# Uniform 128-row value matmuls, paired small matmuls and a planned order per engine in a fused sliding-window attention and token mixer

## Chip, cores and metric

The kernel runs on one core of one Trainium2 chip. The metric is the device time of one execution in microseconds (us), lower is better. Most figures are the median of several executions. An execution is called slow here when it is over 1.5% longer than the fastest of the same kernel.

## The reference

For 8 batches and 8 heads, with 576 tokens and 64 numbers a head, attention looks back over 128 tokens and has a bias that falls with distance. Its output, heads side by side, is `x` (576 x 512 for each batch), which goes through a token mixer.

```python
scores = scale * np.matmul(q, k.transpose(0, 1, 3, 2))
mask = (rel >= 0) & (rel < window)                     # window = 128
scores = np.where(mask, scores + bias[None], -1e9)
attn = softmax(scores)                                 # over the last axis
x = np.matmul(attn, v)                                 # then heads side by side: (8, 576, 512)

wq = x @ w_q                                           # 576 x 64
wk = x @ w_k                                           # 576 x 64
W_tok = scale * np.einsum('bsd,btd->bst', wq, wk)
mixed = np.einsum('bst,btd->bsd', W_tok, x)            # = scale * wq (wk^T x)
out = np.maximum(mixed, 0.0) @ w_out
```

Both kernels use the form in the last comment: `G = wk^T x` (64 x 512) first, then `wq G`. So no 576 x 576 matrix is made in the mixer.

## The kernel before

The kernel is software-pipelined by hand. Each unit of work is put on a list with a time; the list is sorted and issued in that order, and each engine then works through its own part strictly in order. The units of one batch, with the names used below:

- `c.q`, `c.k`, `c.v`: GpSimd casts the loaded fp32 data to fp16. `T` and `eT`: TensorE transposes q and k, and an eviction copies them out of PSUM.
- `QK.u` (8 a batch), `exp.u` on ScalarE, `mul.u` on VectorE: scores, exponent, and an in-place multiply with a table of the bias and mask.
- `PV.t` and `nrm.t` (5 a batch): values times weights for a tile of 128 queries, and the division on VectorE. The fifth tile has 64 tokens.
- `xT`, `wq`, `wk`, `G`, `mx`, `out`: the mixer, with evictions `exT`, `ewq`, `ewk`, `eG`, `emx`, `eo`. `st`: stores.

PSUM is used as four buffers of two banks each, shared by all these units.

```python
PERIOD = 16.0
...
    def pv_unit(b, qt, t):
        ...
            for h in range(H):
                o = 512 * (h // 4) + 65 * (h % 4)
                kts = ([qt - 1] if qt else []) + [qt]
                for i, kt in enumerate(kts):
                    g, c = P_AT[kt, qt]
                    kn = QT_N[kt]                       # 128, or 64 for the last tile of keys
                    nc.tensor.matmul(px[:n, o : o + 65], st["p", h, g][:kn, c : c + n],
                                     vb[:kn, kt, h, :],
                                     start=(i == 0), stop=(i == len(kts) - 1))
...
    def wk_unit(b, t):      # wk by tokens: transposes of the projection's eviction
        ...
                nc.tensor.transpose(pk[:n, 64 * i : 64 * i + 64],
                                    st["wqkT"][64:128, 128 * i : 128 * i + n],
                                    identh[64:128, 64:128])
...
    def g_unit(b, t):       # wk^T x, one matmul of 512 columns for each tile of tokens
        ...
                nc.tensor.matmul(pg[0:64, 0:512], st["wkn"][:n, 64 * i : 64 * i + 64],
                                 st["x", i][:n, :], start=(i == 0), stop=(i == NQT - 1))
...
    def mixed_unit(b, db, t, eng):   # four tiles, one after the other
        ...
            for lo, hi in ((0, 512), (512, S)):
                nc.tensor.matmul(pm[:, lo:hi], st["g"][:, 128 * db : 128 * db + 128],
                                 st["wqkT"][0:64, lo:hi], start=True, stop=True)
...
        for u in range(8):
            qk_unit(b, u, t0 + 2.0 * u)
        for qt, t in enumerate((10.4, 12.4, 18.4, 20.4, 22.4)):
            pv_unit(b, qt, t0 + t)
        ...                                             # times written by hand
```

The softmax here doesn't subtract the row's maximum and nothing guards it: scores larger than these inputs give would overflow.

## Time and profile before

| | before |
|---|---|
| median of 3 executions | 206.88 us (205.60 to 207.73) |
| span of the profiled execution | 209.2 us |
| TensorE busy | 170.2 us, 81% |
| VectorE busy | 145.4 us |
| ScalarE busy | 113.9 us |
| GpSimd busy | 86.5 us |

These lines are from the page of the kernel before: busy time by engine (PE is TensorE, PEld its weight loads, DVE VectorE, ACT ScalarE, POOL GpSimd), the chain of waits by engine, and the two groups of bias multiplies (count, busy us, mean ns, idle before them).

```profile
PE 170.2 (81%) x1712; PEld 101.3 (48%) x1712; DVE 145.4 (69%) x246; ACT 113.9 (54%) x129; POOL 86.5 (41%) x142
...
PE 55%; DVE 19%; ACT 6%; DMA 5%; SPq 5%; issue 4%; POOL 3%; DVEq 0%; ACTq 0%; POOLq 0%
...
L229 DVE TENSOR_TENSOR pt<-pt,btab 128x1024 f16<-128x1024 f16 x32 | 27.2, 851 | 5.0 <-ACT pt L216 4.8
...
L223 DVE TENSOR_TENSOR pt<-pt,btab 128x1024 f16<-128x1024 f16 x32 | 25.4, 795 | 3.9 <-ACT pt L216 3.9
```

The whole-span 81% hides the stages. The next lines are windows of the same execution: stretch, its length, busy us of each engine, then the granted clock, the DMA share and GB/s. The last stretch is one whole batch at full clock.

```profile
core 0: us, PE busy (x) PEld busy (x) DVE busy (x) ACT busy (x) POOL busy (x), PEclk, DMA share, GB/s
0.00:60.00 60.00, 35.54 (x390) 23.00 (x391) 41.15 (x61) 33.18 (x40) 38.70 (x74) 0.80 1.10 283
60.00:190.00 130.00, 121.17 (x1251) 72.52 (x1248) 96.32 (x172) 77.01 (x85) 47.78 (x68) 0.95 0.52 149
190.00:209.20 19.20, 13.53 (x76) 5.73 (x76) 7.89 (x13) 3.76 (x5) 0.00 (x0) 0.93 0.35 123
105.65:127.00 21.35, 19.35 (x215) 11.85 (x214) 16.93 (x30) 13.76 (x16) 11.85 (x17) 1.00 0.73 194
```

The start is short of data and of casts, while the middle is bound by TensorE: 121 of 130 us busy, and in one batch of 21.35 us it is idle for 2.0.

The timeline of TensorE in that batch shows where its time goes (start, us from first start to last end, then line, operation and shape). A matmul's end is modelled and overlaps the next one, so the cost of a group is read from the starts of successive groups.

```profile
104.99 0.66 PE L250 MATMUL px<-vnat_67,pt 128*128 128x65 f16 x16
105.48 1.02 PE L384 MATMUL po<-wout_sb,rm 128*128 128x512 f16 x4
...
107.27 2.41 PE L250 MATMUL px<-vnat_67,pt 128*64 128x65 f16 x16
109.61 1.04 PE L384 MATMUL po<-wout_sb,rm 128*128 128x512 f16 x4
```

Sixteen value matmuls of a full tile take 105.48 - 104.99 = 0.49 us. Sixteen of the last tile take 109.61 - 107.27 = 2.34 us, although they have half the output columns: they use 128 and 64 rows of the array in turn (the line shows only the first form).

### The profile page before, as it was taken

The numbers are of one execution on the slowest core, as the hardware profiler recorded it, in microseconds if no ns is written. First come the engines' busy times: TensorE is split into PE (matmuls) and PEld (weight loads), VectorE is DVE, ScalarE is ACT, GpSimd is POOL, SyncE is SP. The second block draws the span as 40 slices with busy tenths as digits, with TensorE's granted clock in tenths as the row PEclk, the third lists the DMA queues.
The fourth block names the chain that finished last, engine by engine and source line by source line (L and its number), as shares of the span: only waits on it lengthen the run. The fifth ranks groups of instructions, "written<-read, shape, count | busy, mean of one in ns | idle before, by whom it ended". The sixth has DMA issues, their size and how long they took to land.

```text
span 209.2 us, 4255 instructions
## 1 busy us (share of the span) xinstructions
PE 170.2 (81%) x1712; PEld 101.3 (48%) x1712; DVE 145.4 (69%) x246; ACT 113.9 (54%) x129; POOL 86.5 (41%) x142
## 2 busy tenths in 40 slices
PE   0664297698399888999798989999899899989891
PEld 0442174455256545565465546564556455546330
DVE  2794259859974799558858886688858865983613
ACT  7093387438146567366665577357755853531050
POOL 4674684986744562756159425920330000000000
PEclk9995579759859999889999999699999996999997
DMA  6999999999999989369964990342012202210506
GB/s 220 355 275 261 284 316 254 304 265 296 318 248 273 263 254 300 96 185 234 311 180 129 259 276 15 97 118 93 3 65 86 78 0 103 100 25 24 201 9 222
DMA packets 52804, 38.68 MB, mean 185 GB/s; under 512 B 39472, under 2 KB 39984, under 8 KB 52784
## 3 DMA queue, kind: packets, MB, share of 16 engines
q1 hardware_dynamic: 51200, 37.75, 64.1%
q0 software_dynamic: 1584, 0.66, 2.5%
q8 instruction: 13, 0.21, 0.4%
q14 instruction: 7, 0.06, 0.1%
HBM read 29.62 MB, written 9.44 MB: 187 GB/s over the span
## 4 chain that ended last, share of the span: by engine, by line
PE 55%; DVE 19%; ACT 6%; DMA 5%; SPq 5%; issue 4%; POOL 3%; DVEq 0%; ACTq 0%; POOLq 0%
PE po L384 16%; PE px L250 13%; PE ps L206 6%; DMA vraw<-in_v_dram 5%; PE ptr L187 5%; SPq L107 4%; PE pxt L283 4%; PE pg L340 4%; DVE pt L229 4%; DVE osb L79 3%; ACT pt L216 3%; PE pw L304 3%; DVE pt L223 3%; PE pm L358 3%; DVE gm L345 2%
## 5 line engine op out<-in xcount | busy, mean ns | idle before, releaser
L216 ACT ACTIVATE pt<-ps 128x1024 f16<-128x1024 f32 x64 | 64.3, 1027 | 15.0 <-PE ps L206 14.4
L384 PE MATMUL po<-wout_sb,rm 128*128 128x512 f16 (+1 forms) x160 | 44.3, 404 | 1.8 <-ACT osb L77 0.6
L250 PEld LDWEIGHTS <-pt 128*128 128x128 f16 (+1 forms) x576 | 30.3, 101 | 15.4 <-issue 8.4
L137 POOL CAST vnat_67<-vraw 128x512 f16<-128x512 f32 (+1 forms) x20 | 17.9, 904 | 35.9 <-PE px L250 29.5
L229 DVE TENSOR_TENSOR pt<-pt,btab 128x1024 f16<-128x1024 f16 x32 | 27.2, 851 | 5.0 <-ACT pt L216 4.8
L137 POOL CAST vnat_66<-vraw 128x512 f16<-128x512 f32 (+1 forms) x20 | 16.9, 850 | 27.7 <-PE px L250 18.8
L223 DVE TENSOR_TENSOR pt<-pt,btab 128x1024 f16<-128x1024 f16 x32 | 25.4, 795 | 3.9 <-ACT pt L216 3.9
L119 POOL CAST qc<-qraw 128x384 f16<-128x384 f32 x48 | 26.0, 576 | 4.2 <-DMA qraw<-in_q_dram 3.9
L258 DVE RECIPROCAL inv<-px 128x8 f32<-128x8 f32 (+1 forms) x40 | 8.0, 200 | 25.5 <-PE px L250 25.5
L119 POOL CAST kc<-kraw 128x384 f16<-128x384 f32 x42 | 23.3, 588 | 0.0
L364 ACT ACTIVATE rm<-pm 128x576 f16<-128x576 f32 x24 | 14.6, 648 | 13.7 <-PE pm L358 13.1
L187 PE MATMUL ptr<-identh,qc 128*128 128x128 f16 x144 | 13.5, 242 | 10.4 <-POOL qc L119 10.1
L384 PEld LDWEIGHTS <-rm 128*128 128x128 f16 (+1 forms) x160 | 14.5, 103 | 15.1 <-issue 3.5
L250 PE MATMUL px<-vnat_66,pt 128*128 128x65 f16 (+2 forms) x288 | 19.8, 203 | 1.8 <-DVE wqkT L309 1.3
L250 PE MATMUL px<-vnat_67,pt 128*128 128x65 f16 (+2 forms) x288 | 19.8, 203 | 1.6 <-DVE xT L288 1.2
L358 PE MATMUL pm<-wqkT,gm 64*128 64x512 f16 x64 | 12.6, 294 | 7.6 <-DVE gm L345 4.3
L187 PE MATMUL ptr<-identh,kc 128*128 128x128 f16 x144 | 13.6, 243 | 6.2 <-POOL kc L119 3.7
L77 ACT COPY qT<-ptr 128x1152 f16<-128x1152 f16 x8 | 9.0, 1119 | 17.3 <-PE ptr L187 17.3
L79 DVE COPY osb<-po 128x1024 f32<-128x1024 f32 (+1 forms) x16 | 15.1, 949 | 4.0 <-PE po L384 3.9
L77 ACT COPY osb<-po 128x1024 f32<-128x1024 f32 x8 | 8.1, 1012 | 17.3 <-PE po L384 17.3
L288 DVE COPY xT<-pxt 128x1024 f16<-128x1024 f16 (+1 forms) x24 | 12.8, 552 | 6.4 <-PE pxt L283 6.2
L187 PEld LDWEIGHTS <-qc 128*128 128x128 f16 x144 | 9.6, 107 | 14.4 <-POOL qc L119 12.4
(202 smaller groups left out, 215.4 us busy)
## 6 DMA issues: line engine op xcount, KB each, us to landing
qraw<-in_q_dram SPq DMA_DIRECT2D x16, 576.0 KB, 7.9
kraw<-in_k_dram SPq DMA_DIRECT2D x16, 576.0 KB, 7.4
vraw<-in_v_dram SPq DMA_DIRECT2D x32, 256.0 KB, 6.9
out_dram<-osb SPq DMA_DIRECT2D x16, 512.0 KB, 3.0
vraw<-in_v_dram SPq DMA_DIRECT2D x8, 128.0 KB, 7.0
out_dram<-osb SPq DMA_DIRECT2D x8, 128.0 KB, 2.6
wout_sb<-in_moe_w_out_dram POOLq DMA_DIRECT2D x1, 512.0 KB, 10.7
wqk_sb<-in_moe_w_q_dram POOLq DMA_DIRECT2D x1, 64.0 KB, 7.3
```

Of the source, the lines that this page charges most:

```text
L77: eng.copy(out_ap, in_ap)
L79: eng.tensor_copy(out=out_ap, in_=in_ap)
L119: eng.tensor_copy(out=st[name + "c", dd][:, lo:hi], in_=st[name + "raw", dd][:, :, lo:hi].rearrange("p t r d -> p r t d"))
L137: nc.gpsimd.tensor_copy(out=vnat[b % 2][:n, kt, :, 1:65], in_=states[b]["vraw"][:n, kt])
L187: nc.tensor.transpose(pt[:, 128 * r : 128 * r + 128], src[:, r].rearrange("p t d -> p (t d)"), identh)
L216: nc.scalar.activation(out=pt.rearrange("p a b -> p (a b)"), in_=st["ps", u], func=AF.Exp, scale=SCALE)
L223: nc.vector.tensor_tensor(out=pt.rearrange("p a (k b) -> p a k b", k=2), in0=pt.rearrange("p a (k b) -> p a k b", k=2), in1=btab[:, sl : s ...
L229: nc.vector.tensor_tensor(out=pt, in0=pt, in1=btab[:, sl : sl + 2, :], op=ALU.mult)
L250: nc.tensor.matmul(px[:n, o : o + 65], st["p", h, g][:kn, c : c + n], vb[:kn, kt, h, :], start=(i == 0), stop=(i == len(kts) - 1))
L358: nc.tensor.matmul(pm[:, lo:hi], st["g"][:, 128 * db : 128 * db + 128], st["wqkT"][0:64, lo:hi], start=True, stop=True)
L364: nc.scalar.activation(out=st["rm"][:, db, :], in_=pm[:, 0:S], func=AF.Relu, scale=WSCALE)
L384: nc.tensor.matmul(po[:n, 512 * i : 512 * i + 512], st["rm"][:, db, 128 * qt : 128 * qt + n], wout_sb[:, db, :], start=(db == 0), stop=(db ...
```

## The change

The intent has three parts. First, value matmuls always take 128 rows: rows of absent keys are zero in `vnat`, so they add nothing. Second, the mixer's small matmuls are reshaped: wk is taken by tokens directly from the transposed x (20 matmuls of 64 columns instead of 5 transposes, and no wait for the projection's eviction), and `wk^T x` and the mixing run two at a time, in the two column halves or row halves of the array. Third, the hand-written times give way to a plan with a time for each unit, and other times for the loads, casts and transposes of the first batches. The eviction of q's first transpose also goes from VectorE to ScalarE (in batch 0 alone, that of q's second goes the other way). The core of the diff, with cuts marked:

```diff
+PLAN = {
+    'G': 30.91, 'PV.0': 15.87, 'PV.1': 19.19, 'PV.2': 19.72, 'PV.3': 22.75, 'PV.4': 24.59,
+    ...
+    'exp.7': 14.32, 'ld.k0': -21.70, ... 'mul.0': 12.54,
+    'mul.1': 3.30, 'mul.2': 13.78, 'mul.3': 12.87, 'mul.4': 9.12, 'mul.5': -0.75, 'mul.6': 8.95,
+    ...
+}
+PLAN_OF = { ('T.k0', 0): -66.07, ... ('ld.v2', 0): 7.93, ... }     # the first two batches
...
+    def at(self, name, b, f):
+        t = PERIOD * b + PLAN_OF.get((name, b), PLAN.get(name, 0.0))
+        self.items.append((t, len(self.items), f))
...                                                                  # pv_unit
-                    kn = QT_N[kt]
-                    nc.tensor.matmul(px[:n, o : o + 65], st["p", h, g][:kn, c : c + n],
-                                     vb[:kn, kt, h, :],
+                    nc.tensor.matmul(px[:n, o : o + 65], st["p", h, g][:, c : c + n],
+                                     vb[:, kt, h, :],
...                                                                  # wk_unit
-                nc.tensor.transpose(pk[:n, 64 * i : 64 * i + 64],
-                                    st["wqkT"][64:128, 128 * i : 128 * i + n],
-                                    identh[64:128, 64:128])
+                for dc in range(4):
+                    nc.tensor.matmul(pk[:, 64 * i : 64 * i + 64],
+                                     st["xT"][:, dc, 128 * i : 128 * i + 128],
+                                     wk_sb[:, dc], start=(dc == 0), stop=(dc == 3))
...                                                                  # g_unit
-                nc.tensor.matmul(pg[0:64, 0:512], st["wkn"][:n, 64 * i : 64 * i + 64],
-                                 st["x", i][:n, :], start=(i == 0), stop=(i == NQT - 1))
+                for c in range(2):
+                    nc.tensor.matmul(pg[64 * c : 64 * c + 64, 0:256],
+                                     st["wkn"][:, 64 * i : 64 * i + 64],
+                                     st["x", i][:, 256 * c : 256 * c + 256],
+                                     start=(i == 0), stop=(i == NQT - 1))
...                                                                  # mixed_unit
+            for i in ((e,) if e < 2 else (0, 1)):
+                for c in range(2):
+                    o, lo, w = (512 * c, 0, 512) if e < 2 else (512 * c + 64 * i, 512, 64)
+                    nc.tensor.matmul(pm[:, o : o + w],
+                                     st["g"][64 * c : 64 * c + 64, 128 * i : 128 * i + 128],
+                                     st["wqT"][64 * c : 64 * c + 64, lo : lo + w],
+                                     start=True, stop=True)
...
-            t_unit(b, name, dd, t0 - 14.4 + 4.0 * i, nc.vector if i == 0 else nc.scalar)
+            t_unit(b, name, dd, nc.vector if b == 0 and i == 2 else nc.scalar)
```

## The prediction

> **What bounds the kernel now.** Median 206.9 us; the profiled span is 209.2 us. The page: TensorE busy 170.2 us (81%), VectorE 145.4, ScalarE 113.9, GpSimd 86.5. By windows: from 0 to 60 us TensorE is busy 35.5 of 60 (DMA at about 285 GB/s, first PV at 26.9 us); from 60 to 190 us 121 of 130; from 190 to 209 us 13.5 of 19. In the chain of waits TensorE has 55%, VectorE 19%. So the middle is bound by TensorE, about 22 us a batch (first output matmuls of successive batches at 59, 82.5, 105, 126.5, 148.5, 168, 186.5, 200 us), of which 19.3 us is work at full clock, 2 to 2.5 us waits, the rest a clock that drops now and then.
>
> **What the change does, per batch** (starts of successive groups, timeline of 104 to 127 us):
> - Last value tile (PV.4): 16 matmuls that alternate 128 and 64 rows take 2.34 us, 146 ns each; 16 of a full tile take 0.49 us, 31 ns each. The Trainium skill, "TensorEngine Tiling (Array Packing)", Tiling Modes, Key Properties, says that a change of tiling mode drains the array; 146 against 31 ns agrees. With 128 rows no mode changes inside; still 64 columns wide, so I take 0.9 us (estimate): saves 1.4.
> - Mixing: 4 x (512+64) columns singly, 4 x about 0.36 us. In pairs on two row tiles, as QK already runs (6 matmuls in 0.33 us): about 0.7. Saves 0.75.
> - wk^T x: 5 x 512 columns take 1.3 us; ten of 256 in column pairs about 0.7. Saves 0.6.
> - wk: 5 transposes (0.36 us) become 20 matmuls of 64 columns, at PV's 31 to 35 ns about 0.65. Costs 0.3, but wk no longer waits for the projection's eviction.
> - Last x^T: no mode changes, about -0.1.
> TensorE: about 2.6 us less, so 16.7 us a batch at full clock.
> - VectorE loses one qT eviction (1.35), part of a relu (0.75 becomes 0.3), 0.3 of the g eviction: about 2 us less, 15.3 a batch. Its bias multiplies (0.68 us alone, mean 0.8, up to 2.8 while GpSimd casts) remain.
> - ScalarE gains the qT eviction (1.12); relu 3 x 0.65 becomes 2 x 1.0: about 14.9 a batch.
> - New load order in the first two batches: first PV at about 22 instead of 27 us, PV.2 bound by DMA (about 7 MB ahead of it).
>
> **On the critical path.** In the middle nearly all of the 2.6 us, since TensorE is the bound. But then TensorE (16.7), VectorE (15.3), ScalarE (14.9) and DMA (4.7 MB a batch at 285 GB/s: 16.6 us) stand close together in fixed order, so waits stay at about 2 us: I estimate 18 to 19 us a batch. First output at about 54 us instead of 59, middle batches 3 to 3.5 us less each, start and tail the rest. Sum: about 28 us less.
>
> **Prediction: 179 us, 170 to 189 (8 in 10).** Faster by over 2%: 0.95; within 2%: 0.03; slower: 0.02.
>
> **What would show it.** PV.4's group at 0.7 to 1.1 us; mixing's pairs starting together; TensorE busy about 148 us; middle batches 18 to 19 us apart; VectorE about 130, ScalarE about 122 us busy; both larger in the chain of waits.
>
> **What would make it wrong.** 64-column loads in PV.4 near 100 ns; pairs in mixing or wk^T x not overlapping; the planned order stalling one engine behind another (a period of 20+: about 190 us); GpSimd casts stretching the multiplies; a colder clock from more idle TensorE. On the good side, an order that fits so well that the period is 17: about 171 us.

## The result and the profile after

| | before | after |
|---|---|---|
| median | 206.24 us (4 executions) | 168.80 us (4 executions) |
| every execution | 203.11, 205.60, 206.88, 207.73 | 164.97, 165.08, 172.51, 180.77 |
| ratio of fast runs | | 0.8076 (95%: 0.7863 to 0.8288) |
| TensorE / VectorE / ScalarE busy | 170.2 / 145.4 / 113.9 us | 141.2 / 142.5 / 122.1 us |
| span of the profiled execution | 209.2 us | 179.0 us |

A ratio is the mean time of one kernel's fast runs over that of the other's fast runs of the same rounds, so it is not quite the ratio of the medians in the table. The change is clearly faster, and more so than forecast: the median lies just below the predicted range of 170 to 189. The executions are spread over 16 us, which the kernel before does not show, and the profiled one is the slowest.

Page lines of the kernel after that answer to those of before:

```profile
PE 141.2 (79%) x1872; PEld 92.0 (51%) x1872; DVE 142.5 (80%) x237; ACT 122.1 (68%) x128; POOL 77.2 (43%) x143
...
PE 35%; DVE 25%; DMA 15%; issue 11%; POOL 6%; SPq 3%; ACT 2%; DVEq 1%; POOLq 0%
...
L278 DVE TENSOR_TENSOR pt<-pt,btab 128x1024 f16<-128x1024 f16 x32 | 38.9, 1237 | 0.0
...
L284 DVE TENSOR_TENSOR pt<-pt,btab 128x1024 f16<-128x1024 f16 x32 | 25.5, 801 | 3.8 <-ACT pt L271 3.8
```

TensorE lost 29 us of work. VectorE lost only 3, although it has less to do: the 32 multiplies of one form went from 795 to 1237 ns in the mean (this form was line 223 before and is line 278 now).

The windows of the kernel after show the start up to the first output matmul, and then three batches:

```profile
core 0: us, PE busy (x) PEld busy (x) DVE busy (x) ACT busy (x) POOL busy (x), PEclk, DMA share, GB/s
0.00:49.00 49.00, 32.47 (x454) 24.23 (x455) 33.16 (x66) 38.86 (x45) 34.06 (x63) 0.90 1.06 289
73.63:90.30 16.67, 16.20 (x237) 10.68 (x235) 14.12 (x28) 14.99 (x16) 6.87 (x15) 1.00 0.72 198
90.30:115.13 24.83, 17.70 (x237) 11.41 (x235) 23.14 (x28) 14.92 (x16) 9.87 (x20) 0.86 0.85 250
115.13:131.60 16.47, 16.23 (x238) 10.70 (x236) 14.56 (x28) 15.13 (x16) 8.88 (x17) 1.00 0.69 182
```

There are two kinds of batch. The usual one takes 16.5 us with TensorE busy for 16.2, so almost no wait is left. The other takes 8 us more, with VectorE busy for 23 us of it. The profiled execution has two of these (49.0 to 73.6 us is the other), and 179.0 less twice 8 is the 163 us that the fast executions span.

The last value tile, in TensorE's timeline of the kernel after:

```profile
88.06 0.65 PE L304 MATMUL px<-vnat_67,pt 128*128 128x65 f16 x16
88.57 0.66 PE L242 MATMUL ptr<-identh,kc 128*128 128x128 f16 x9
89.17 0.69 PE L304 MATMUL px<-vnat_67,pt 128*64 128x65 f16 x16
89.79 0.68 PE L242 MATMUL ptr<-identh,qc 128*128 128x128 f16 x9
```

Its 16 matmuls now take 89.79 - 89.17 = 0.62 us instead of 2.34.

And the first of the two long batches, in the timeline of all engines (lines of weight loads, DMA issues and ScalarE are left out):

```profile
56.54 2.14 POOL L184 CAST vnat_66<-vraw 64x512 f16<-64x512 f32 x3 [4.84 <-DMA vraw<-in_v_dram]
...
57.25 0.69 DVE L316 TENSOR_TENSOR x_1056<-px,inv 128x512 f16<-128x512 f32 x1
...
57.86 7.90 DVE L278 TENSOR_TENSOR pt<-pt,btab 128x1024 f16<-128x1024 f16 x1
...
59.14 0.39 PE L417 MATMUL pm<-wqT,gm 64*128 64x512 f16 x2
...
59.65 1.40 POOL L166 CAST kc<-kraw 128x384 f16<-128x384 f32 x3
...
64.27 0.50 POOL L166 CAST kc<-kraw 128x384 f16<-128x384 f32 x1
64.72 0.50 POOL L166 CAST qc<-qraw 128x384 f16<-128x384 f32 x1
65.68 0.41 DVE L430 TENSOR_SCALAR rm<-pm 128x256 f16<-128x256 f32 x1
...
66.15 0.38 PE L304 MATMUL px<-vnat_66,pt 128*128 128x65 f16 x4 [6.62 <-DVE rm L430]
```

GpSimd gets its v data at 56.5 us and runs 17 casts without a pause until 65.2. One bias multiply, `mul.1` of the next batch, starts on VectorE at 57.86, inside that burst, and takes 7.90 us where it takes 0.68 alone. It ends at 65.76, 0.5 us after the last cast of the burst, so about one undisturbed multiply later. Behind it on VectorE stands an eviction of the mixing; TensorE has its next matmuls (`PV.1`) waiting for that, for 6.62 us, and its granted clock is 0.86 in the windows of both long batches (90.30 to 115.13 above, and 49.00 to 73.63), against 1.00 in the usual ones.

### The profile page after: what moved, and what is told of

It is laid out like the page before. It is cut to its first block, busy times and chain, and to the rows that moved or that the text cites. A ratio compares the mean times of both kernels' runs of the same rounds, so it can differ in the third digit from the quotient of the medians.

```text
span 179.0 us, 4518 instructions
## 1 busy us (share of the span) xinstructions
PE 141.2 (79%) x1872; PEld 92.0 (51%) x1872; DVE 142.5 (80%) x237; ACT 122.1 (68%) x128; POOL 77.2 (43%) x143
## 4 chain that ended last, share of the span: by engine, by line
PE 35%; DVE 25%; DMA 15%; issue 11%; POOL 6%; SPq 3%; ACT 2%; DVEq 1%; POOLq 0%
DMA vraw<-in_v_dram 15%; PE po L450 14%; DVE pt L278 10%; PE px L304 9%; DVE pt L284 4%; PE pxt L337 4%; PE ps L261 4%; SPq L154 3%; PE ptr L242 3%; DVE xT_76 L341 2%; POOL vnat_66 L184 2%; POOL vnat_67 L184 2%; DVE wqT L363 1%; POOL kc L166 1%; DVE wkn L381 1%
## 5 line engine op out<-in xcount | busy, mean ns | idle before, releaser
L271 ACT ACTIVATE pt<-ps 128x1024 f16<-128x1024 f32 x64 | 62.4, 1036 | 28.4 <-PE ps L261 27.8
L450 PE MATMUL po<-wout_sb,rm 128*128 128x512 f16 (+1 forms) x160 | 42.0, 390 | 0.1
L278 DVE TENSOR_TENSOR pt<-pt,btab 128x1024 f16<-128x1024 f16 x32 | 38.9, 1237 | 0.0
L304 PEld LDWEIGHTS <-pt 128*128 128x128 f16 (+1 forms) x576 | 23.5, 107 | 23.0 <-issue 19.6
L184 POOL CAST vnat_67<-vraw 128x512 f16<-128x512 f32 (+1 forms) x20 | 13.0, 674 | 50.4 <-DMA vraw<-in_v_dram 36.9
L304 PE MATMUL px<-vnat_66,pt 128*128 128x65 f16 (+1 forms) x288 | 14.6, 213 | 18.6 <-DVE rm L430 14.5
L284 DVE TENSOR_TENSOR pt<-pt,btab 128x1024 f16<-128x1024 f16 x32 | 25.5, 801 | 3.8 <-ACT pt L271 3.8
L184 POOL CAST vnat_66<-vraw 128x512 f16<-128x512 f32 (+1 forms) x20 | 14.2, 728 | 24.8 <-DMA vraw<-in_v_dram 24.8
L426 ACT ACTIVATE rm<-pm 128x1024 f16<-128x1024 f32 x16 | 15.7, 1025 | 7.6 <-PE pm L417 7.6
L122 DVE COPY osb<-po 128x1024 f32<-128x1024 f32 (+1 forms) x16 | 15.1, 947 | 6.7 <-PE po L450 6.5
L120 ACT COPY qT<-ptr 128x1152 f16<-128x1152 f16 x15 | 17.0, 1132 | 3.2 <-PE ptr L242 2.7
L261 PE MATMUL ps<-qT,kT_69 64*128 64x256 f16 (+2 forms) x160 | 13.0, 272 | 1.0 <-ACT pt L271 0.8
L261 PE MATMUL ps<-qT,kT_68 64*128 64x256 f16 (+2 forms) x160 | 12.5, 265 | 1.4 <-ACT pt L271 0.9
L304 PE MATMUL px<-vnat_67,pt 128*128 128x65 f16 (+1 forms) x288 | 12.0, 194 | 1.1 <-POOL vnat_67 L184 0.7
L242 PEld LDWEIGHTS <-kc 128*128 128x128 f16 x144 | 9.8, 108 | 3.8 <-DVE kc L166 2.1
```

The lines of the kernel that those rows point to most:

```text
L120: eng.copy(out_ap, in_ap)
L122: eng.tensor_copy(out=out_ap, in_=in_ap)
L184: nc.gpsimd.tensor_copy(out=vnat[b % 2][:n, kt, :, 1:65], in_=states[b]["vraw"][:n, kt])
L242: nc.tensor.transpose(pt[:, 128 * r : 128 * r + 128], src[:, r].rearrange("p t d -> p (t d)"), identh)
L261: nc.tensor.matmul(ps[:, 512 * i + o : 512 * i + o + w], st["kT"][64 * i : 64 * i + 64, dd, h2, 128 * kb : 128 * kb + 128], st["qT"][64 * ...
L271: nc.scalar.activation(out=pt.rearrange("p a b -> p (a b)"), in_=st["ps", u], func=AF.Exp, scale=SCALE)
```

## The experiments

Theory P ("port stalls" in the expectations) explains the spread of the new kernel: a multiply with both inputs in SBUF can be held by GpSimd's casts. Its rival is that the spread comes with the granted clock or with DMA. Theory A explains the gain: TensorE's work sets the time of a batch, so the new shapes are the gain. Its rival B is that waits between engines set it, so the plan is.

### 1 to 3: the changed kernel again, and one multiply moved

Edit of `e2_mul1_late` (`e3_mul1_mid` has 4.40 instead of 8.94; `e1_after_again` is the changed kernel unchanged):

```diff
         t = PERIOD * b + PLAN_OF.get((name, b), PLAN.get(name, 0.0))
+        if name == "mul.1" and b:
+            t = PERIOD * b + 8.94
```

> The changed kernel unchanged, for its spread and a second trace. Theory (port stalls): its time is about 165 us plus about 8 us for each time that one bias multiply (mul.1) starts just after a burst of GpSimd casts has begun and is held for the whole burst (7.8 us twice in the 180.8 us execution). So times should fall in steps near 165, 172 and 180 us, and a fast execution has no multiply over 3 us. Rival (clock): the times spread evenly with the granted clock, and a slow execution has all its matmuls a little longer.

> The same, but mul.1 of each batch from the second on stands later on VectorE, behind the norm of tile 3, at the end of the stretch without multiplies. Port stalls: nothing is left to be held at the start of the burst, so every execution is near 164 us (162 to 167) and none at 172 or 180; no multiply over 4 us. Rival (clock or DMA): the spread 165 to 180 stays.

> The same, but mul.1 stands two VectorE evictions later (about 2 us), where the burst has surely begun. Port stalls: it is held for 6 to 8 us in nearly every batch from the third on, so 190 to 210 us. Rival: moving one 0.6 us multiply by 2 us changes nothing, 165 to 180 us.

| run | median | every execution, sorted |
|---|---|---|
| e1, unchanged | 181.02 us | 163.95, 172.91, 180.17, 181.86, 182.09, 182.19 |
| e2, mul.1 late | 164.92 us | 163.73, 164.41, 164.81, 165.02, 165.04, 165.41 |
| e3, mul.1 mid | 172.54 us | 171.49, 171.86, 172.21, 172.54, 177.69, 178.48, 178.76 |

The kernel before, in the same rounds, has a median of 206.05 us. The ratio of e2 to it is 0.8018 (0.7977 to 0.8059).

The levels near 164, 172 and 181 us are there, with nothing between. The trace of e1, a slow execution, has again two multiplies held:

```profile
42.77 7.99 DVE L278 TENSOR_TENSOR pt<-pt,btab 128x1024 f16<-128x1024 f16 x1
...
66.66 7.93 DVE L278 TENSOR_TENSOR pt<-pt,btab 128x1024 f16<-128x1024 f16 x1
```

In e2 all six executions lie within 1.7 us, and in its profiled one the longest multiply takes 2.78 us:

```profile
49.10 2.78 DVE L280 TENSOR_TENSOR pt<-pt,btab 128x1024 f16<-128x1024 f16 x1
```

So the slow executions are not a state of the chip: moving one 0.6 us multiply to the end of VectorE's stretch without multiplies takes them away. The granted clock alone would not have told this, since it goes with the time (0.963 at 163.95 us, 0.950 at 172.91, 0.913 to 0.923 at 180 to 182). But in the slow trace of the changed kernel the usual batches have the full clock and take 16.5 to 16.7 us, like those of e2 (16.2 to 17.0); only the batches with a hold are longer. The level at 172 us was never profiled; that it has one hold is inferred from the steps.

The strong form of theory P fell with e3. I expected a multiply placed surely inside the burst to be held in nearly every batch, for 190 to 210 us. In the profiled execution (177.69 us) only two were held for long, 6.15 and 5.41 us, and the seven executions took 171 to 179. So standing inside a burst makes a hold possible, not certain.

The usual batch of e2, in three windows:

```profile
core 0: us, PE busy (x) PEld busy (x) DVE busy (x) ACT busy (x) POOL busy (x), PEclk, DMA share, GB/s
67.34:83.53 16.19, 16.09 (x237) 10.54 (x235) 14.03 (x28) 15.05 (x16) 7.15 (x15) 1.00 0.90 265
83.53:100.54 17.01, 16.36 (x237) 10.45 (x235) 15.52 (x28) 15.09 (x16) 8.48 (x19) 1.00 1.05 295
100.54:117.35 16.81, 16.35 (x237) 10.44 (x235) 15.32 (x28) 15.08 (x16) 9.83 (x20) 1.00 0.90 254
```

The mean is 50.01 / 3 = 16.7 us a batch with TensorE busy for 16.3. This form, without long holds, is the base for the experiments that undo a part of the change.

### 4: the hold by itself

`e4_lock_alone` gives wrong results on purpose. One multiply is let go by a GpSimd cast, with more GpSimd work queued behind that cast; the tag `a` stands for casts and two SBUF inputs, `m` for memsets instead of casts, `p` for one input in PSUM, `s` for one SBUF input and a constant.

```diff
+        nc.gpsimd.tensor_copy(out=go[:, 0:384], in_=raw[:, 0:384])
+        for i in range(n):                                  # n = 0, 1, 2, 4, 8, 16
+            nc.gpsimd.tensor_copy(out=sink[i], in_=raw[:, 0:384])   # or a memset of sink[i]
+        nc.vector.tensor_tensor(out=res, in0=go, in1=tab, op=ALU.mult)
+        nc.vector.tensor_copy(out=raw[:, 0:8], in_=res[:, 0:8])
```

> A kernel with wrong results on purpose: one fp16 multiply on VectorE is let go when a GpSimd cast ends, while 0, 1, 2, 4, 8 or 16 more casts (0.46 us each) are queued on GpSimd. Port stalls: with two operands in SBUF its time is 0.6 us plus that of ALL the queued casts (16: about 7.9 us), so the port is not handed over between casts. Rival (it waits for one cast only): at most about 1.1 us whatever the number. With 16 memsets on GpSimd in place of casts (no read of SBUF), or with one operand in PSUM: about 0.6 to 1.2 us. The form with one SBUF operand and a constant is left open.

VectorE's timeline: with no more cast queued, with 16 casts, with 16 memsets (and the small copy that follows), and with one input in PSUM and 16 casts.

```profile
5.31 0.69 DVE L139 TENSOR_TENSOR res_a<-go_a,tab 128x1024 f16<-128x1024 f16 x1 [0.60 <-POOL go_a L132]
...
23.99 0.96 DVE L139 TENSOR_TENSOR res_a<-go_a,tab 128x1024 f16<-128x1024 f16 x1 [0.60 <-POOL go_a L132]
...
38.64 0.69 DVE L139 TENSOR_TENSOR res_m<-go_m,tab 128x1024 f16<-128x1024 f16 x1 [0.60 <-POOL go_m L132]
39.37 5.02 DVE L144 CAST raw<-res_m 128x8 f32<-128x8 f16 x1
...
51.73 1.22 DVE L141 TENSOR_TENSOR res_p<-go_p,ps 128x1024 f16<-128x1024 f16 x1 [0.60 <-POOL go_p L132]
```

The expectation was wrong for the main case: with 1, 2, 4, 8 or 16 casts queued the multiply takes 0.96 us each time, so it waits for the running cast only. The form with one SBUF input and a constant does the same: 0.43 us alone, 0.70 with 4 or 16 casts. The other forms are as expected: memsets don't touch the multiply (0.69), and with one input in PSUM it takes 1.22 us with 0, 4 or 16 casts beside it. One line was not expected at all: a copy of 8 columns from fp16 to fp32, SBUF to SBUF, takes 5.02 us behind 16 memsets, where its like takes 0.17. It ends at 44.39 us and the memsets end at 44.35. With 4 memsets it takes 0.70 us and again ends with them. (Not all of the 5.02 us is lost to VectorE: its next instruction starts at 43.47.) So VectorE can lose to a whole run of GpSimd instructions; this probe shows it for a copy against memsets, not for the multiply against casts.

### 5 and 6: the new shapes in the old order

`e5_before_pv128` makes one change to the kernel before; `e6_before_all_math` has all matmul shapes of the new kernel with the hand-written times of the old.

```diff
-                    kn = QT_N[kt]
-                    nc.tensor.matmul(px[:n, o : o + 65], st["p", h, g][:kn, c : c + n],
-                                     vb[:kn, kt, h, :],
+                    nc.tensor.matmul(px[:n, o : o + 65], st["p", h, g][:, c : c + n],
+                                     vb[:, kt, h, :],
...
+            nc.vector.memset(t[64:128, 4], 0.0)
```

> The kernel before, with only the last value tile's matmuls on 128 rows. In the trace of after the 16 matmuls take 0.62 us instead of 2.34 us. Theory A (TensorE's own work sets the period in the old order): eight times 1.7 us less, about 192 us (190 to 196). Rival B (waits between engines set it, so the plan is the gain): at most 4 us less, 202 us or more.

> The old hand-made order with all the new matmul shapes (128-row value tiles, wk by tokens, paired wk^T x and paired mixing with their evictions), old load order, q's first transpose still evicted on VectorE. Theory A: TensorE does about 2.9 us less a batch, so about 184 us (180 to 188). Rival B: 195 us or more, the rest being the plan.

Medians: 193.18 us (192.15 to 196.02) and 186.26 us (185.00 to 188.30), with the kernel before at 205.88 in the same rounds. Ratios of fast runs: 0.9419 (0.929 to 0.9549) and 0.9078 (0.894 to 0.9216). Both fall where theory A put them. The 128-row values alone are worth about 12.7 us by the medians and 11.5 by the means of the fast executions (204.4 and 192.8), against eight times 1.72 us, 13.8: most of what TensorE saves, the kernel saves. The rest of the new shapes adds 6.9 (7.0 by the fast ones). The last value tile in e5:

```profile
101.16 0.69 PE L250 MATMUL px<-vnat,pt 128*64 128x65 f16 x16
101.78 1.04 PE L384 MATMUL po<-wout_sb,rm 128*128 128x512 f16 x4
```

Its 16 matmuls take 0.62 us with nothing else changed.

Windows of three batches of e6:

```profile
core 0: us, PE busy (x) PEld busy (x) DVE busy (x) ACT busy (x) POOL busy (x), PEclk, DMA share, GB/s
77.48:96.74 19.26, 16.98 (x241) 10.87 (x238) 16.17 (x29) 13.70 (x15) 11.31 (x17) 1.00 0.97 272
96.74:115.71 18.97, 17.03 (x241) 10.91 (x237) 17.00 (x29) 13.81 (x15) 11.51 (x17) 1.00 0.82 229
115.71:133.78 18.07, 17.02 (x241) 10.90 (x237) 16.21 (x29) 13.60 (x15) 8.99 (x14) 1.00 0.35 94
```

That is 56.30 / 3 = 18.8 us a batch, TensorE busy for 17.0 of it: in the old order 1.8 us of waits stay. The first output matmul comes at 58.5 us. This profile is of e6's slowest execution (188.30 us). The profiled one of e14 below, which has the same order and is a fast one (186.35), agrees: four batches from 55.19 to 131.39 take 19.05 us each, with TensorE busy for 17.1.

### 7 and 8: the old shapes in the new order

`e7_late_old_pv` is e2 with the value matmuls of before (the reverse of the diff of e5). `e8_late_old_math` is e2 with all matmul shapes of before; since wk then needs the projection's eviction, I moved `wk` and `G` a little later and gave mixing four tiles:

```diff
-    'G': 30.91, ... 'wk': 29.30, 'wq': 29.42, ... 'mx.0': 34.76, 'mx.1': 33.33, 'mx.2': 33.64,
+    'G': 31.95, ... 'wk': 30.87, 'wq': 29.30, ... 'mx.0': 33.33, 'mx.1': 33.64, 'mx.2': 34.70, 'mx.3': 34.80,
```

> The new order with mul.1 late (the form without long stalls, 164.9 us), but the last value tile again with 128 and 64 rows in turn. Theory A (TensorE is still the bound in the new order, with about half a us of slack a batch): 10 to 13 us more, 175 to 178 us. Rival: TensorE has slack now and other engines bind: at most 5 us more, below 170 us.

> The new order with mul.1 late, with all matmul shapes of before (projection first, then wk by transposes, single mixing in four tiles). Theory A: about 2.8 us more a batch, 185 to 190 us, so the plan alone is worth 16 to 20 us and the shapes 20 to 25. Rival B (the plan is nearly the whole gain): below 175 us. A third: the plan without the shapes stalls and is no better than before, 200 us or more.

e7: 181.05 us (179.16 to 185.77), ratio 0.8813 (0.8658 to 0.8968). That is more than theory A gave (175 to 178). The profiled execution is the slowest (185.77): its undisturbed batches take 17.9 us, as theory A has it, and one with a multiply of 2.50 us takes 19.5; but a multiply is held for 5.16 us in the start and the first output comes at 59.7 us instead of 50. What makes the fast ones (179 to 182) longer than theory A was not traced.

e8: 213.04 us (205.56, 209.26, 216.83, 217.77), no faster than before. That is the third option. Its undisturbed batches take 20.5 and 20.8 us with TensorE busy for 19.1, and in the profiled execution (216.83, a slow one) three multiplies are held, for 4.36, 7.45 and 6.13 us. So the plan alone is worth nothing here; it fits the new shapes. How much of this is due to my own places for the old units I can't tell.

### 9: the burst held back instead of the multiply

`e9_gate` leaves mul.1 where the plan has it. GpSimd copies one column of its output before each burst from batch 1 on, so the burst can't begin earlier; a few plan times are shifted to keep every engine's order.

```diff
+    def hold(b):
+        def f():
+            nc.gpsimd.tensor_copy(out=gate, in_=states[b + 1]["pt", 1][:, 0, 0:1])
+        return f
+    for b in range(1, NB - 1):
+        prog.first(PERIOD * b + 19.31, hold(b))             # just before c.v4, c.v1, c.v2
```

> The changed kernel with mul.1 where it was; instead, from batch 1 on, GpSimd copies one column of mul.1's output just before the burst of casts, so the burst cannot begin before mul.1 is done. Port stalls: the two or three discrete levels vanish: one level, 164 to 169 us (the casts of v come up to 2 us later, which may cost a little), no multiply over 4 us. Rival (the late place of mul.1 on VectorE helped for another reason, such as PSUM being freed earlier): 172 and 180 us stay in the list.

168.92 us (168.22 to 169.56), ratio 0.8224 (0.8174 to 0.8273); the longest multiply is 2.99 us. One level, as theory P has it, reached from the other side: no unit on VectorE changed its place. It is 4 us slower than e2. In the window from 85.25 to 102.58 us TensorE waits 0.35 us for a cast of v, which it doesn't in e2, and 0.49 us for a norm (0.40 in e2); and in five batches the last multiply before the output takes 2.99 or 2.52 us behind casts. How the 4 us divide between these was not tested.

### 10, 12 and 13: what makes a multiply wait for the whole burst

Three more probes with wrong results. Each runs the kernel's own burst of 17 casts 16 to 28 times and lets one multiply go at a moment that slides by about 50 ns. In `e10_lock_sweep` VectorE is idle before the multiply; in `e12_lock_behind` another VectorE instruction stands directly ahead of it; in `e13_lock_like` the casts use the kernel's strided forms and separate tiles, with four loads of 576 KB beside each burst.

```diff
+    BURST = "vvvcvcccccccccvcc"                             # v: cast of v, c: cast of k or q
+        nc.scalar.copy(delay[:, 0:cols], wide[:, 0:cols])   # cols = 64 + 60 n: the moment
+        nc.vector.tensor_tensor(out=res, in0=delay[:, 0:1024], in1=tab, op=ALU.mult)    # e10
```

> Wrong results on purpose. Sixteen times the kernel's own burst of 17 casts (v and k or q forms, 8.3 us), with one multiply let go by ScalarE at a moment that moves by about 50 ns from one to the next. The first probe (multiply let go at the edge of a cast) waited for one cast only. If the moment of arrival within a cast decides, some of the sixteen take 5 to 8 us and others under 1.2 us, in a pattern that follows the moment. If it needs something else of the kernel (other VectorE work, DMA), all sixteen stay under 1.5 us.

> Wrong results on purpose. The same burst of 17 casts and the same sliding moment, but the multiply stands directly behind another VectorE instruction, as in the kernel: 16 times behind a norm (one input in PSUM) in mul.1's form, 8 times in the plain form, 4 times behind an instruction with both inputs in SBUF. In the sweep before, a multiply that came to an idle VectorE waited for the running cast only, in all 16. If being queued behind another instruction is what makes it lose again and again, several of these take 4 to 8 us, at moments that depend on the phase. If none is over 1.5 us, the probes do not contain the cause of the long holds, and it stays open.

> Wrong results on purpose. The same probe once more, nearer to the kernel: the casts read the strided forms and separate tiles of the kernel, and four loads of 576 KB run beside each burst. Two probes found a wait of one cast in all 44 tries. If access forms or DMA traffic beside are what lets a multiply lose to a whole burst, several of these 24 take over 3 us. If none does, the long holds are a fact of the kernel's traces that no probe here reproduces, and what decides them stays open.

No multiply was held for a burst. All 16 of e10 take 0.69 to 1.13 us, all 28 of e12 at most 1.10, all 24 of e13 at most 1.03. The wait falls with the moment of arrival as the rest of the running cast does: in e10 a multiply that arrives 83 ns into a cast of v takes 1071 ns, at 283 ns 871, at 483 ns 692. Two such lines of e10:

```profile
14.04 1.07 DVE L143 TENSOR_TENSOR res<-delay,tab 128x1024 f16<-128x1024 f16 x1 [1.16 <-ACT delay L142]
...
89.90 0.69 DVE L143 TENSOR_TENSOR res<-delay,tab 128x1024 f16<-128x1024 f16 x1 [1.55 <-ACT delay L142]
```

So in these probes neither the moment, nor an instruction ahead, nor access forms with DMA beside made the long hold. In all but the first try of each series the multiply arrived in the second to fourth cast of the burst, as the one held in the kernel did (second). In the kernel's trace the multiply at 57.86 us arrives 340 ns into a cast and loses to 15 further casts, and a multiply of the same kind at 42.44 us arrives 405 ns into a cast and loses to no further one. What decides between them stays open.

It is not a choice between one cast and the whole burst, either. The traces hold cases in between, and the kernel before has them too:

```profile
50.75 2.89 DVE L229 TENSOR_TENSOR pt<-pt,btab 128x1024 f16<-128x1024 f16 x1
53.04 1.06 POOL L137 CAST vnat_67<-vraw 128x512 f16<-128x512 f32 x1
```

This multiply waits for the running cast and five more, and then goes ahead of a cast of v, which takes 1.06 us instead of the 0.60 of a like one at 55.41. In e7 and e8 a multiply waits for the running cast and nine or eight more (5.16 and 4.36 us), and the burst goes on behind it.

### 11: three loads moved

```diff
+        if (name, b) in (("ld.v2", 0), ("ld.q0", 3), ("ld.q1", 3)):
+            t = {("ld.v2", 0): 0.95, ("ld.q0", 3): 31.60, ("ld.q1", 3): 31.65}[name, b]
```

> The form with mul.1 late, and three loads moved: the third v tile of batch 0 ahead of q of batch 2, q of batch 3 behind the v tiles of batch 1. In the trace of after, PV.2 of batch 0 waits 2.2 us for that v tile and GpSimd 3.2 us for v of batch 1. If the start is bound by these landings: 1 to 3 us less than 164.9, 162 to 164 us. If the start is bound by the amount of data (about 290 GB/s) or by the order of casts: no change.

165.06 us (164.14 to 165.52 in four executions, 169.63 and 171.37 in two), ratio 0.8019 (0.7944 to 0.8094). A miss: the median is that of e2. In its trace PV.2 of the first batch no longer waits for its v tile (2.02 us in e2), yet the first output comes at 50.9 us, against 50.0; so these landings don't bound the start. And two executions are slow again, so the late place of mul.1 does not give one level with every order of loads. I have no trace of a slow one, so whether they have a hold is not known.

### 14: the old order with the eviction on ScalarE

```diff
-            t_unit(b, name, dd, nc.vector if i == 0 else nc.scalar)
+            t_unit(b, name, dd, nc.vector if b == 0 and i == 2 else nc.scalar)
```

> The old order with all new shapes (186.3 us) and the transposes of q evicted on ScalarE as in the changed kernel (1.35 us a batch less on VectorE, 1.12 more on ScalarE). If balance of work between engines is what the plan brought, 175 us or less; if the order itself is (what stands behind what in each queue), at most 4 us less, 182 to 187 us.

186.44 us (185.28 to 189.44), ratio 0.9076 (0.8823 to 0.9329): the same as e6. Moving 1.35 us a batch from VectorE to ScalarE is worth nothing in the old order; in the new one it was not tested. That leaves, by elimination, the order itself as the plan's gain: which unit stands behind which in each engine's queue, and in which order loads are issued. These two were not built apart. By the profiles of e6 and e2, 8.5 of the 22.8 us between their spans come before the first output (58.5 and 50.0 us). But an earlier start is no gain by itself: e14's first output comes at 55.2, and its time is that of e6.

## Why the prediction was wrong, and where it was right

By cause: 206 us before; the new shapes bring it to 186 (e6); the plan brings it from there to 165 (e2, or the fast executions of the changed kernel); holds of a multiply put 8 us on it each, none, one (inferred) or two times in an execution. The shares hold for this way round only: in the old shapes the plan brings nothing (e8).

- **TensorE bounds the middle: right.** e5 gives back 12.7 of the 13.8 us that its matmuls save (11.5 by the fast executions).
- **The terms of TensorE's work: right, a little too high.** Predicted 16.7 us a batch, measured 16.3 busy. PV.4: 0.9 predicted, 0.62 measured. wk: 0.65 and 0.59. `wk^T x`: 0.7 and 0.67. Mixing: 0.7 and 0.79 (0.47 for the first six matmuls, 0.32 for the last two). The whole was forecast too high as well: TensorE busy about 148 us, measured 141.2 (139.0 in e2).
- **ScalarE 14.9 us a batch: right** (15.1 in the windows of e2). **VectorE 15.3: right** where nothing is held (15.0).
- **The start: first PV at 22 us: right** (22.27), and PV.2 of the first batch waits 2.18 us for its v tile from DMA, as forecast. First output at 54 us: it came at 49, 4 to 5 us earlier.
- **"so waits stay at about 2 us: I estimate 18 to 19 us a batch": this is the step that failed.** The waits came down to 0.4 us (16.7 us a batch with 16.3 of work, in e2). The estimate of 18 to 19 us is what the *old* order gives with the new shapes: 18.8 us with 1.8 us of waits, in e6. Of the 2.1 us a batch between e6 and e2, 1.4 are waits and 0.7 is TensorE's own busy time, 17.0 and 16.3 us for the same matmul shapes; what in the order makes these 0.7 was not looked into. I counted the plan as worth the start only, and took it that engines which all have about 15 us of work in a batch of 16 to 17 must get in each other's way. As an estimate, six batches at 16.7 instead of 18.5 are 11 us and the earlier first output is 4, together the distance from 179 to 164. The prediction had named this case as its good side: a period of 17 and about 171 us.
- **"GpSimd casts stretching the multiplies more": right as a risk, and larger than meant.** It is what makes the 172 and 180 us executions. The typical time of the changed kernel in the second series, 181 us, lies in the predicted range, but not for the predicted reason: its undisturbed batches take 16.2 to 17.1 us in the trace of e1, not 18.5, and the rest is holds: that the number fits is luck.
- **Busy time of VectorE 130 us: wrong for the profiled execution (142.5)** and right for e2 (128.4): the difference is time in which a held multiply counts as busy.

What stays open: what decides whether a multiply that arrives in a burst of casts waits for one cast, for several or for all. That it happens, and that it makes the slow executions, is shown from both sides (e2, e9). How it happens is not: 68 tries in three probes waited for one cast at most.

e2 is the version to keep: as fast as the best executions of the changed kernel, in all six executions (164.9 us median against 168.8 and 181.0 in two series of the changed kernel).

## What to carry to other kernels

When a change brings both cheaper work and a new order, predict them apart: here the waits of the old order, 1.8 us a batch, fell to 0.4 in the planned one, and a build with the old order and the new shapes is a cheap way to separate them. When the executions of one kernel fall into steps of equal size, look for one instruction that is stretched in the slow trace before blaming the clock; its busy time is then waiting in disguise. Where a trace shows such holds, keep VectorE instructions with two SBUF inputs out of the stretches in which GpSimd runs many casts without a pause, or make the burst wait for them.

## What the Trainium skill lacked or had wrong

- "SBUF — State Buffer", Summary: rules for kernel authors, says that where a VectorE instruction has two SBUF inputs and the GpSimd instruction reads SBUF, the second one to issue "fully blocks" until the first finishes. For a multiply with two SBUF inputs the probes agree: 0.69 us alone, 0.96 with casts queued, never more than the rest of one cast. The page doesn't say that the loser can lose again and again: in the kernel a multiply of 0.68 us was held by 15 further casts and took 7.90 us, and in a probe a copy of 8 columns (0.17 us) took 5.02 us beside a run of 16 memsets.
- A check, not a lack: Who interferes with whom, on the same page, says that a multiply with one input in PSUM, or GpSimd work that doesn't read SBUF, doesn't contend. The probes agree: 1.22 us with 0, 4 or 16 casts, and 0.69 us with 0, 4 or 16 memsets.
- "TensorEngine Tiling (Array Packing)", Tiling Modes, Key Properties, says that a change of mode drains the array, without a figure. Here 16 value matmuls that alternate between 128 and 64 rows cost 146 ns each, and 39 ns each with 128 rows throughout.
- "TensorE: Matmul & The Clock Gate", LDWEIGHTS (loading the stationary operand), gives a load as columns / 1.2 ns, which makes 53 ns for 64 columns. Pairs of a 64-column load and a 65-column matmul started 39 ns apart in the last value tile (0.62 us for 16), so that figure is too high as a cost per pair here. The record of one such load is 106 to 113 ns long; the loads overlap.
